# Moving the FFN token sums, a norm and the exps of Strassen groups to later slots of the program

## The chip, the cores and the metric

The kernel runs on one core of one Trainium2 chip. The metric is the device time of one execution in microseconds. Executions of one kernel lie within 0.5 to 4 us of each other here, so differences of one or two microseconds are judged from several rounds with an interval, not from single runs. The span that a profile shows is about 1.7 us shorter than the time of the same execution.

An engine (PE = TensorE, DVE = VectorE, ACT = ScalarE, POOL = GpSimd) runs its instructions in program order in these traces: in before, a sum that waited 5.28 us at the head of DVE's queue held up all DVE work behind it. SP issues nearly all DMA transfers of this kernel, also in program order (f4 below swaps two in the program, and the trace swaps them too), so a transfer whose data is not ready holds up those behind it.

## The reference

Two blocks, each behind a layer norm, on 2048 tokens of width 1024:

```
h  = x + linear_attention(layernorm(x)) @ wo        # 32 heads, phi(t) = where(t > 0, t+1, exp(t)) + 1e-6
h2 = h + (relu(g) * u) @ W_down                     # g, u = layernorm(h) @ W_gate, W_up ; width 3584
```

## The kernel before

The kernel is one long program in five stages: key/value projections, query projections, output projection (mixed with late attention tiles), gate and up products, down product. Most products use a Strassen scheme: seven products for eight, paid with sums of the operands and of the results. One group `sgroup` of seven products:

```python
a, f, b = alloc_bank(pool), alloc_bank(pool), alloc_bank(pool)
prod(a, X(0, 0), W(0, 0), True, "P1");  ident_act(bank(b), bank(a), ...)      # fk1: ACT copies PSUM to PSUM
hook(1)                                   # work of the group before (pend[1]), then a hook of the caller
prod(f, SX(2), TW(2), True, "P7");      ident_act(atmp, bank(f), ...)         # s7
hook(2)
... P6 -> fk2, hook(3), P2 -> e11 (exp on ACT, then min/add and max on DVE), hook(4) ...
prod(c, SX(0), TW(0), False, "P5");     ident_act(btmp[:, 0, :], bank(c), ...)  # sc
s22 = e22(...);  s22[0]()                 # DVE add
hook(5)
prod(b, X(1, 1), TW(3), False, "P4")
for f_ in s22[1:2]: f_()                  # exp of block (1,1), on ACT
s21 = e21(...);  s21[0]()                 # DVE add
for f_ in s22[2:]: f_()                   # min/add and max of block (1,1), on DVE
hook(6)
prod(c, SX(3), W(1, 1), False, "P3")
pend[1] = list(e12(...));  pend[2] = list(s21[1:2]);  pend[3] = list(s21[2:])
hook(7)
```

For keys and queries the four results go through phi; for values they are copied or added. A k group and a v group alternate; layer norms and operand sums of later tiles hang on the v group's hooks.

The output projection stage. `a2(t)` is the attention of a tile: matmuls, three DVE operations, then the transpose DMA T3d. `a4(t)` is the projection of a tile: 16 matmuls, residual add on DVE into a ring of three, store of h, then for the first eight tiles the statistics on ACT (two passes) and a chain of five small POOL operations. `a4_norm` is the norm on ACT and the transpose DMA T5d into `hnT`, the FFN's input. `s_sums` are the four Strassen sums over all of `hnT`, on DVE.

```python
LAG = NE                                   # 4
for t in range(NE, NST + LAG + 1):
    if LAG + 1 <= t < TPP + LAG + 1:
        a4_norm(t - LAG - 1)               # ACT norm, then T5d on SP
    if LAG <= t < NST + LAG:
        a4(t - LAG)
    if t < NST:
        a2(t)                              # ends with T3d on SP, read four steps later by a4(t)
    if t in (5, 7, 9, 11, 18, 19):
        load_w_next()                      # 512 KB of FFN weights, on SP
    if t >= 9:
        run(pool_t, 1)
    if 13 <= t < 17:
        s_sums()[t - 13]()
```

## Time and profile before

| | before |
|---|---|
| time, median | 761.73 us (761.55 to 762.08) |
| PE busy | 740.7 of 761.0 us |
| keys and values, to the first query product | 124.14 us |
| queries | 55.89 us (to 180.03) |
| output projection, to the first FFN product | 69.66 us (to 249.69) |
| FFN, to the end | 511.3 us |

Stage borders are read from the timeline of PE as starts of the first matmul with the next stage's tiles. The head and busy line of the page of before, and the engine shares of the chain that ended last:

```profile
span 761.0 us, 10079 instructions
PE 740.7 (97%) x3547; PEld 337.8 (44%) x3603; DVE 548.3 (72%) x1083; ACT 293.8 (39%) x500; POOL 84.5 (11%) x148
PE 89%; DVE 5%; ACT 3%; issue 2%; DMA 1%; DVEq 0%; POOL 0%; ACTq 0%; SPq 0%; POOLq 0%
```

PE is busy nearly always, so the change can only win PE's idle time and what PE loses at a lowered clock. The largest piece is in the projection stage. Timeline of before for PE there. The columns of a timeline are start and duration in us, engine, source line, operation, output<-input, shape, count, and in brackets the idle time in front and who ended it:

```profile
220.64 3.63 PE L602 MATMUL ps<-RW,RE 128*128 128x512 bf16 x15 [1.27 <-DMA RE<-RE]
...
224.62 3.63 PE L602 MATMUL ps<-RW,RE 128*128 128x512 bf16 x16
232.73 1.06 PE L602 MATMUL ps<-kvz,RAB 128*128 128x132 bf16 x8 [4.48 <-DVE RE L989]
```

RE<-RE is the attention transpose T3d. The long gap waits for DVE's line 989, an attention eviction. Timelines of before for DVE, ACT and the DMA queue of SP tell why that was late; line 1084 is a token sum, L1047 the norm, RH<-RXH its transpose T5d:

```profile
221.62 1.23 DVE L989 TENSOR_TENSOR RE<-ps,rden 128x1024 bf16<-128x1024 f32 x1
228.13 1.60 DVE L1084 TENSOR_TENSOR RC<-RH 128x2048 f16<-128x2048 bf16 x1 [5.28 <-DMA RH<-RXH]
...
218.18 1.24 ACT L1047 ACTIVATE RXH<-RXH,s 128x1024 bf16<-128x1024 bf16 x1 [1.43 <-POOL s L1037]
223.07 1.24 ACT L1047 ACTIVATE RXH<-RXH,s 128x1024 bf16<-128x1024 bf16 x1 [1.43 <-POOL s L1037]
...
224.34 1.24 SPq L512 DMA_TRANSPOSE RH<-RXH  x1
```

The sum stood at the head of DVE's queue 5.28 us, waiting for the last transpose. ACT's norms come every 4.89 us (223.07 minus 218.18), against 3.92 us of PE work per tile, because each norm waits 1.43 us for POOL. The windows view of before (window, busy time of each engine, PEclk, DMA share, GB/s) shows what the gap did to PE's clock:

```profile
227.04:230.96 3.92, 1.21 (x6) 0.36 (x4) 2.83 (x3) 0.00 (x0) 3.62 (x3) 1.00 1.14 249
230.96:234.88 3.92, 2.15 (x12) 1.32 (x13) 3.78 (x6) 0.00 (x0) 0.00 (x0) 0.55 1.06 309
234.88:238.80 3.92, 3.87 (x11) 1.49 (x11) 2.87 (x5) 0.00 (x0) 0.00 (x0) 0.57 1.08 235
```

A "busy" PE at a granted clock of 0.55 does little more than half the work. The Trainium skill ("TensorE: Matmul & The Clock Gate", Part 1) describes just this: an idle window halves the clock until the array has been busy for a while; the trace agrees: in windows of 0.1 us the clock is 0.50 from 231.39 to 238.22, which is 6.83 us.

In the key/value stage DVE has hardly any slack. DVE of before at the start of a v group (the v group's first product starts on PE at 73.28); the second and third line are the min/add and the max of a phi:

```profile
73.35 0.69 DVE L839 TENSOR_TENSOR RX<-ps,RXH 128x512 f32<-128x512 f32 x1
74.01 0.29 DVE L644 TENSOR_SCALAR RX<-RX 128x512 bf16<-128x512 bf16 x1
74.34 0.69 DVE L647 SCALAR_TENSOR_TENSOR RE<-RX 128x512 bf16<-128x512 f32 x1
75.52 0.29 DVE L644 TENSOR_SCALAR RX<-RX 128x512 bf16<-128x512 bf16 x1 [0.49 <-ACT RX L640]
```

And PE's waits of before between 60 and 110 us (total, times, longest):

```profile
PE ps L602 <- ACT RX L607: 2.2, 2, 1.3
PE ps L602 <- ACT ps L607: 0.7, 2, 0.4
```

### The profile page before, as it was taken

How to read it: one execution, taken by the hardware profiler on the slowest of the kernel's cores; microseconds unless marked ns; L12 is line 12 of the kernel's file. 1: busy time of each engine (PE TensorE's matmuls, PEld its weight loads, DVE VectorE, ACT ScalarE, POOL GpSimd, SP SyncE). 2: the span in 40 equal slices, each digit the busy share in tenths (PEclk: the TensorE clock that was granted, in tenths of full speed). 3: DMA queues.
4: the chain of work that ended last, by engine and by line, in shares of the span. 5: the costliest groups of instructions: out<-in, count | busy, mean ns of one | idle time of the engine just before them, and what ended most of it. 6: DMA issues, size and time to landing. Idle time of an engine off the chain costs nothing.

```text
span 761.0 us, 10079 instructions
## 1 busy us (share of the span) xinstructions
PE 740.7 (97%) x3547; PEld 337.8 (44%) x3603; DVE 548.3 (72%) x1083; ACT 293.8 (39%) x500; POOL 84.5 (11%) x148
## 2 busy tenths in 40 slices
PE   8999899999997999999999999999999999999998
PEld 3444344344543444444444444444444444444443
DVE  7978985889757698888886665847667686653343
ACT  4345455665650445454544100024454544420000
POOL 2656720000261000000000000000000000000000
PEclk9999999999998999999999999999999999999999
DMA  9643104212997777556545699753132332026664
GB/s 302 195 95 73 41 15 161 103 29 55 216 215 193 241 233 217 173 176 185 158 138 166 210 269 294 214 188 111 56 111 70 97 100 67 1 73 181 208 190 137
DMA packets 160225, 113.38 MB, mean 149 GB/s; under 512 B 51504, under 2 KB 141360, under 8 KB 160176
## 3 DMA queue, kind: packets, MB, share of 16 engines
q1 hardware_dynamic: 160176, 112.75, 51.5%
q8 instruction: 28, 0.46, 0.3%
q14 instruction: 21, 0.17, 0.1%
HBM read 85.46 MB, written 15.73 MB: 133 GB/s over the span
## 4 chain that ended last, share of the span: by engine, by line
PE 89%; DVE 5%; ACT 3%; issue 2%; DMA 1%; DVEq 0%; POOL 0%; ACTq 0%; SPq 0%; POOLq 0%
PE ps L602 89%; ACT ps L607 1%; ACT RX L640 1%; DVE RAB L647 1%; DVE RX L644 1%; DVE RX L839 1%; DVE RWG L764 1%; DMA RE<-RE 1%; ACT RXH L607 0%; DVE RE L900 0%; DVE RE L989 0%; DVE RXH L1008 0%; DVE st L615 0%; DVE rden L987 0%; DVE RXH L629 0%
## 5 line engine op out<-in xcount | busy, mean ns | idle before, releaser
L607 ACT ACTIVATE ps<-ps 128x512 f32<-128x512 f32 x150 | 87.5, 584 | 173.0 <-PE ps L602 155.6
L602 PE MATMUL ps<-RC,RO 128*128 128x512 f16 x672 | 154.2, 379 | 0.0
L602 PE MATMUL ps<-RW,RAB 128*128 128x512 f16 (+1 forms) x681 | 150.1, 379 | 0.6
L602 PEld LDWEIGHTS ps<-RW,RAB 128*128 128x128 bf16 (+1 forms) x692 | 67.7, 98 | 81.7
L602 PE MATMUL ps<-RH,RWG 128*128 128x512 bf16 x435 | 103.0, 379 | 0.7
L602 PEld LDWEIGHTS ps<-RC,RO 128*128 128x128 f16 x672 | 65.7, 98 | 79.3
L607 ACT ACTIVATE RE<-ps 128x512 f32<-128x512 f32 x120 | 71.1, 598 | 76.7 <-PE ps L602 54.5
L602 PE MATMUL ps<-RC,RWG 128*128 128x512 f16 x296 | 70.9, 379 | 0.7 <-ACT ps L607 0.7
L602 PEld LDWEIGHTS ps<-RH,RWG 128*128 128x128 bf16 x448 | 43.8, 98 | 52.9
L1171 DVE TENSOR_TENSOR RAB<-ps,RAB 128x512 bf16<-128x512 f32 x28 | 19.3, 691 | 65.1 <-PE ps L602 65.1
L602 PE MATMUL ps<-RW,RE 128*128 128x512 bf16 x248 | 59.1, 390 | 2.1 <-DMA RE<-RE 1.3
L602 PE MATMUL ps<-RH,RO 128*128 128x512 bf16 (+1 forms) x242 | 58.3, 379 | 0.7
L602 PE MATMUL ps<-RAB 128*128 128x512 bf16 x239 | 56.7, 379 | 1.3 <-ACT RAB L691 0.7
L607 ACT ACTIVATE RAB<-ps 128x512 bf16<-128x512 f32 x56 | 33.4, 597 | 62.0 <-PE ps L602 62.0
L1102 DVE TENSOR_TENSOR RO<-RWG,RO 128x512 f16<-128x512 bf16 x108 | 45.5, 421 | 1.8
L623 POOL TENSOR_TENSOR rstd<-ve,neghalf 128x1 f32<-128x1 f32 x24 | 14.8, 615 | 276.9 <-DVE ve L620 276.9
L602 PEld LDWEIGHTS ps<-RC,RWG 128*128 128x128 bf16 (+1 forms) x296 | 28.5, 98 | 36.6 <-ACT ps L607 3.1
L1178 DVE TENSOR_TENSOR RE<-ps,RE 128x512 f32<-128x512 f32 x56 | 38.4, 691 | 5.0 <-ACT RE L607 5.0
L615 DVE BATCH_NORM_STATS2 st<-RE 128x6 f32<-128x512 bf16 x48 | 30.7, 681 | 13.9 <-DMA RE<-h_scr 13.1
L1102 DVE TENSOR_TENSOR RO<-RWG 128x512 f16<-128x512 bf16 x108 | 40.7, 418 | 0.0
L602 PEld LDWEIGHTS ps<-RW,RE 128*128 128x128 bf16 x256 | 25.0, 100 | 31.3 <-issue 3.0
L602 PEld LDWEIGHTS ps<-RH,RO 128*128 128x128 f16 (+1 forms) x256 | 24.5, 98 | 31.1 <-ACT RX L607 2.6
(112 smaller groups left out, 808.1 us busy)
## 6 DMA issues: line engine op xcount, KB each, us to landing
RWG<-in_B_W_gate_dram SPq DMA_DIRECT2D x28, 512.0 KB, 3.7
RWG<-in_B_W_up_dram SPq DMA_DIRECT2D x28, 512.0 KB, 4.7
RW<-t_scr SPq DMA_DIRECT2D x56, 256.0 KB, 3.3
RW<-in_B_W_down_dram SPq DMA_DIRECT2D x42, 256.0 KB, 4.3
RW<-in_B_W_down_dram SPq DMA_DIRECT2D x14, 512.0 KB, 3.9
t_scr<-RW SPq DMA_DIRECT2D x14, 512.0 KB, 4.8
RE<-in_A_x_dram SPq DMA_DIRECT2D x23, 256.0 KB, 4.1
RAB<-in_A_wqkv_dram SPq DMA_DIRECT2D x8, 512.0 KB, 8.2
```

The source lines that it names most:

```text
L602: lambda e: e.matmul(out_ap, lhsT, rhs, start=start, stop=stop, skip_group_check=skip),
L607: PL.add("act", lambda e: e.activation(out=dst, in_=src, func=func), reads=reads, writes=writes, name=name)
L615: PL.add("dve", lambda e, c=c: e.bn_stats(out=st6[:, k, c * 6:(c + 1) * 6], in_=src_full[:, c * BCH:(c + 1) * BCH]), reads=[src_chunk_bufs ...
L623: PL.add("pool", lambda e: e.tensor_tensor(out=rstd[:, k, :], in0=ve[:, k, :], in1=neghalf[:], op=ALU.pow), reads=[B_ve[k], B_neghalf], wr ...
L640: PL.add("act", lambda e: e.activation(out=Et[:, k, :], in_=src, func=ACTF.Exp), reads=[src_buf], writes=[B_E[k]], name=name + "_exp")
L644: PL.add("dve", lambda e: e.tensor_scalar(out=Et[:, k, :], in0=Et[:, k, :], scalar1=1.0, scalar2=1e-6, op0=ALU.min, op1=ALU.add), reads=[] ...
L647: PL.add("dve", lambda e: e.scalar_tensor_tensor(out=dst_ap, in0=src, scalar=C1, in1=Et[:, k, :], op0=ALU.add, op1=ALU.max), reads=[src_bu ...
L764: PL.add("dve", lambda e: e.tensor_tensor(out=s(i), in0=in0, in1=in1, op=op), reads=reads, writes=[B_Sx[i][p]], name="Sx%d_%d" % (i + 1, p))
L839: PL.add("dve", lambda e: e.tensor_tensor(out=tmp, in0=p_, in1=s_, op=ALU.add), reads=[pb, sb_], writes=[tmp_buf], name=name + "_add")
L1102: PL.add(eng, lambda e: e.tensor_tensor(out=Tring[:, k, j], in0=in0, in1=in1, op=ALU.subtract), reads=reads, writes=[B_T[k][j]], name="T%d ...
L1171: PL.add("dve", lambda e: e.tensor_tensor(out=hh[:, f1, 0:SBW], in0=bank(BA[1]), in1=r11[:, rr, :], op=ALU.mult), reads=[B_bank[BA[1]], B_ ...
L1178: PL.add("dve", lambda e, w=w: e.tensor_tensor(out=ftmp[:, 4 + w, :], in0=bank(BF_[w]), in1=ftmp[:, 2 + w, :], op=ALU.add), reads=[B_bank[ ...
```

## The change

Its intent: let no engine wait at the head of its queue for something that will be ready a little later. Three parts, cut to the core (names of temporaries follow from it: s7 alternates between two buffers so that sums can be made in place):

```diff
 # 1. exps of a group issued in the next group's slots
-            ident_act(atmp, bank(f), [B_bank[f]], [B_at], name + "s7")
+            grp[0] += 1
+            s7, b7 = [(atmp, B_at), (btmp[:, 1, :], B_bt[1])][grp[0] % 2]
+            ident_act(s7, bank(f), [B_bank[f]], [b7], name + "s7")
...
             prod(b, X(1, 1), TW(3), False, "P4")
-            for f_ in s22[1:2]:
-                f_()
             s21[0]()
-            for f_ in s22[2:]:
-                f_()
...
-            pend[2] = list(s21[1:2])
-            pend[3] = list(s21[2:])
+            pend[2] = list(s22[1:])
+            pend[3] = list(s21[1:])
...
-                    hooks[3] = kvfin
+                    hooks[6] = kvfin
                 if r == 1:
-                    hooks[5 if ct == 0 else 3] = lambda t=ct: a2(t)
+                    hooks[6] = lambda t=ct: a2(t)
 # 2. norm of a tile behind the next one's statistics
+            if LAG <= t < NST + LAG:
+                a4(t - LAG)
             if LAG + 1 <= t < TPP + LAG + 1:
                 a4_norm(t - LAG - 1)
-            if LAG <= t < NST + LAG:
-                a4(t - LAG)
 # 3. token sums two tiles later
-            if 13 <= t < 17:
-                s_sums()[t - 13]()
+            if 15 <= t < 19:
+                s_sums()[t - 15]()
```

More of the change, by code (lines that the diff above doesn't have):

```diff
@@ L798, in sgroup @@
             prod(f, SX(2), TW(2), True, "P7")
-            ident_act(atmp, bank(f), [B_bank[f]], [B_at], name + "s7")
+            grp[0] += 1
+            s7, b7 = [(atmp, B_at), (btmp[:, 1, :], B_bt[1])][grp[0] % 2]
+            sc, bc = btmp[:, 0, :], B_bt[0]
+            ident_act(s7, bank(f), [B_bank[f]], [b7], name + "s7")
             hook(2)
@@ L809, in sgroup @@
             prod(c, SX(0), TW(0), False, "P5")
-            ident_act(btmp[:, 0, :], bank(c), [B_bank[c]], [B_bt[0]], name + "sc")
-            s22 = e22(bank(f), B_bank[f], btmp[:, 0, :], B_bt[0])
+            ident_act(sc, bank(c), [B_bank[c]], [bc], name + "sc")
+            s22 = e22(bank(f), B_bank[f], sc, bc)
             s22[0]()
@@ L814, in sgroup @@
             prod(b, X(1, 1), TW(3), False, "P4")
-            for f_ in s22[1:2]:
-                f_()
-            s21 = e21(bank(b), B_bank[b], atmp, B_at)
+            s21 = e21(bank(b), B_bank[b], s7, b7)
             s21[0]()
-            for f_ in s22[2:]:
-                f_()
             hook(6)
@@ L823, in sgroup @@
             pend[1] = list(e12(bank(c), B_bank[c]))
-            pend[2] = list(s21[1:2])
-            pend[3] = list(s21[2:])
+            pend[2] = list(s22[1:])
+            pend[3] = list(s21[1:])
             hook(7)
         pend = {}
+        grp = [0]
         def flush():
@@ L834, in flush, with add_phi @@
             pend.clear()
-        def add_phi(dst, dst_buf, tmp, tmp_buf, name):
+        def add_phi(dst, dst_buf, name):
             def go(p_, pb, s_, sb_):
                 def add():
-                    PL.add("dve", lambda e: e.tensor_tensor(out=tmp, in0=p_, in1=s_, op=ALU.add), reads=[pb, sb_],
-                           writes=[tmp_buf], name=name + "_add")
-                return (add,) + phi_steps(tmp, tmp_buf, dst, dst_buf, name)
+                    PL.add("dve", lambda e: e.tensor_tensor(out=s_, in0=p_, in1=s_, op=ALU.add), reads=[pb],
+                           writes=[sb_], name=name + "_add")
+                return (add,) + phi_steps(s_, sb_, dst, dst_buf, name)
             return go
@@ L889, in k_group @@
             sgroup(P1_POOL, True, X, SX, W, TW, pl(0, 0), pl(0, 1),
-                   add_phi(*dst(1, 0), btmp[:, 0, :], B_bt[0], "k_%d_0" % (2 * p + 1)),
-                   add_phi(*dst(1, 1), btmp[:, 1, :], B_bt[1], "k_%d_1" % (2 * p + 1)), "k%d" % p, hooks)
+                   add_phi(*dst(1, 0), "k_%d_0" % (2 * p + 1)),
+                   add_phi(*dst(1, 1), "k_%d_1" % (2 * p + 1)), "k%d" % p, hooks)
         def v_group(p, hooks=()):
@@ L932, in q_group @@
             sgroup(A_POOL[r], False, X, SX, W, TW, pl(0, 0), pl(0, 1),
-                   add_phi(*dst(1, 0), btmp[:, 0, :], B_bt[0], "q_%d_%d" % (r, ct)),
-                   add_phi(*dst(1, 1), btmp[:, 1, :], B_bt[1], "q_%d_%d" % (r, ct)), "q%d%d" % (r, ct), hooks)
+                   add_phi(*dst(1, 0), "q_%d_%d" % (r, ct)),
+                   add_phi(*dst(1, 1), "q_%d_%d" % (r, ct)), "q%d%d" % (r, ct), hooks)
         kv_started = [False] * 8
```

## The prediction

> **What bounds the kernel.** TensorE. The busy table gives PE 740.7 of 761.0 us (97%); the chain of waits is 89% PE. From about 249.5 us on (the FFN) the PE runs in regular 12.03-us pairs without gaps, and the change does not touch that. So only idle time before 249.5 us can be won, and all the change can win is far below 20 us.
>
> **Where PE idles (timeline and windows).**
> 1. Output projection + late attention, 180.0 to 249.5 us. Its matmuls need about 60.8 us (256 x 0.216 + 12 x 0.46) but take 69.5. One gap of 4.48 us stands at 228 us, released by DVE (L989): DVE had waited 5.28 us for the transpose DMA that completes hnT, at the head of its in-order queue with the first FFN token sum (1.60 us), and the projection's evictions stood behind it. After the gap the granted clock is 0.55 to 0.57 for about 8 us, as the Trainium skill says of an idle window ("TensorE: Matmul & The Clock Gate", Part 1); the trace agrees. Another 1.27-us gap (219 us) waits for a transpose.
> 2. Both come from ScalarE: each norm waits 1.43 us for the GpSimd chain of its own statistics, so a tile costs ACT 4.89 us against 3.92 us of PE, and T5d, then T3d on the same DMA queue fall behind.
> 3. Query groups, 124 to 180 us: about 4 us over the pure matmul time; DVE 8.3 to 9.5 of 10 us busy.
> 4. Key/value groups, 67 to 104 us: two pairs of 15.3 and 15.65 us instead of 13.5; DVE 9.3 to 9.65 of 10 busy.
>
> **What the change does.** No operation is added or removed; DVE, ACT and PE busy time should stay within 1%.
> - Norm behind the next statistics: ACT needs about 3.46 us per tile, so it keeps pace with PE; the last norm ends near 217 us instead of 224.3, hnT is complete near 221 instead of 228.1. Transposes for the projection are issued earlier.
> - Sums two tiles later: the first one starts near 229.5 us, hnT already there. The 4.5-us gap, the clock dip and most of the 1.27-us gap go: about -8.5 us. DMA is near full there (share 0.8 to 1.1), so a stall of a microsecond may remain.
> - Exps deferred: fk1 no longer waits behind the exp of the previous group. But fk2 still stands behind four ScalarE operations (0.25 us per query group stays), and DVE's work in the second half of the queries (about 7.06 us per group against 6.5 of PE) is the same, only its backlog moves into the projection. Query phase: -0.5 to -1.
> - Keys/values: the last min/add + max of each k group (0.98 us) moves into the v group, where DVE has 8 to 9 us of work, and leaves DVE idle about 1 us longer at the v group's start. There DVE is the limit, so this costs 0.5 to 0.8 us in each of three pairs: +1.5.
>
> **Sum:** 761.9 - 8.5 - 0.8 + 1.2 = about 753.8 us, range 750.0 to 757.5. Chances: faster by over 2% 0.05, within 2% 0.94, slower 0.01.
>
> **Signs.** Right: no DVE wait on the hnT transpose, no PE gap over 2 us after 180 us, clock 1.0 throughout, FFN start near 241 to 243 us, ACT no longer waiting 1.43 us on GpSimd per tile, pairs of the FFN still 12.03 us. The key/value pairs 0.5 us or more longer.
> **Wrong if:** transposes land later under the denser DMA traffic (PE waits on RE<-RE), the key/value deferral costs or wins several us, or hnT comes later than 229 us.

## The result

The changed kernel takes 759.1 us at the median (758.46 to 759.78) against 761.73. The ratio is 0.9965 (0.9948 to 0.9982). Ratios here are the mean time of one kernel's fast runs over that of the other's of the same rounds, so not quite the ratio of the quoted medians. That is 2.6 us won where about 8 were predicted, and outside the predicted range.

| stage, from the PE timelines | before | after | difference | predicted |
|---|---|---|---|---|
| keys and values | 124.14 | 126.46 | +2.3 | +1.2 (+1.5 in the text) |
| queries | 55.89 | 54.56 | -1.3 | -0.8 |
| output projection | 69.66 | 64.43 | -5.2 | -8.5 |
| FFN | 511.3 | 511.35 | 0 | 0 |
| span | 761.0 | 756.8 | -4.2 | -8.1 |

The profile of before happened to catch an execution of 762.71 us with the long clock dip (mean clock 0.995), that of after one of 758.46, the fastest of its four, so the differences of the table add up to 1.6 us more than the medians do. The page of after:

```profile
span 756.8 us, 10080 instructions
PE 737.7 (97%) x3547; PEld 337.2 (45%) x3603; DVE 545.6 (72%) x1083; ACT 291.2 (38%) x500; POOL 82.3 (11%) x148
```

Busy times are nearly the same: within 1%, but for POOL. Of the 4.2 us of span, 3.0 are PE's busy time, matmuls that no longer run at half clock (mean clock 1.0), and 1.2 are PE's idle time. In the projection stage the long gap is gone, the first sum starts at 232.35 without any wait, and the norms no longer wait for POOL, except the last one, 0.29 us instead of 1.43. PE, DVE and ACT of after:

```profile
221.75 3.63 PE L602 MATMUL ps<-RW,RE 128*128 128x512 bf16 x15 [0.60 <-DMA RE<-RE]
...
230.98 3.63 PE L602 MATMUL ps<-RW,RE 128*128 128x512 bf16 x15 [1.21 <-DMA RE<-RE]
235.09 10.52 PE L602 MATMUL ps<-RW,RE 128*128 128x512 bf16 x47 [0.49 <-DMA RE<-RE]
245.45 1.89 PE L602 MATMUL ps<-RH,RWG 128*128 128x512 bf16 x8
...
232.35 1.22 DVE L1084 TENSOR_TENSOR RC<-RH 128x2048 f16<-128x2048 bf16 x1
...
217.78 1.24 ACT L1047 ACTIVATE RXH<-RXH,s 128x1024 bf16<-128x1024 bf16 x1 [0.29 <-POOL s L1037]
```

PE waits for attention transposes instead. Why they are late shows in SP's queue of after. The last norm ended at 219.02, yet its transpose was issued at 224.80:

```profile
219.71 0.58 SPq L508 DMA_DIRECT2D h_scr<-RXH  x1
220.34 1.30 SPq L512 DMA_TRANSPOSE RH<-RXH  x1
221.75 1.25 SPq L512 DMA_TRANSPOSE RE<-RE  x1
223.04 0.58 SPq L508 DMA_DIRECT2D RWG<-in_B_W_up_dram  x1
223.72 0.56 SPq L508 DMA_DIRECT2D RE<-in_A_x_dram  x1
224.33 0.43 SPq L508 DMA_DIRECT2D h_scr<-RXH  x1
224.80 1.51 SPq L512 DMA_TRANSPOSE RH<-RXH  x1
226.42 2.49 SPq L512 DMA_TRANSPOSE RE<-RE  x1
```

Each issue follows the one before without a pause. From T3d of tile 6 to T3d of tile 12 (199.96 to 226.42 us) SP took 4.41 us per tile and was busy for 95% of that stretch; before, it was 4.95 us per tile, at 73%. The issues have also become longer: the last one above takes 2.49 us, where T3d took 1.29 to 1.68 in the same tiles of before. The last T5d landed 5.3 us after its issue began, at 230.1 us, against 228.1 before.

In the key/value stage, DVE of after at the start of the same v group (here the v group's first product starts at 74.00):

```profile
74.31 0.68 DVE L839 TENSOR_TENSOR RXH<-ps,RXH 128x512 f32<-128x512 f32 x1
76.23 0.29 DVE L644 TENSOR_SCALAR RX<-RX 128x512 bf16<-128x512 bf16 x1 [1.24 <-ACT RX L640]
...
79.82 0.76 DVE L644 TENSOR_SCALAR RX<-RX 128x512 bf16<-128x512 bf16 x1
80.61 1.11 DVE L647 SCALAR_TENSOR_TENSOR RE<-RXH,RX 128x512 bf16<-128x512 f32 x1
```

DVE idles 1.24 us where before it did a min/add and a max and idled 0.49. One more such pair now stands later in the v group, where POOL is busy: the pair at 79.82 takes 0.76 + 1.11 us, the same work took 0.29 + 0.69 us at 74.01 in the profile of before. The Trainium skill ("SBUF — State Buffer", "SBUF: two separate sides") says that DVE operations of certain kinds and GpSimd operations lock each other out of a shared port. The longer durations beside a busy POOL agree with that in part (the min/add at 76.23 took 0.29 us although POOL's records show it busy then too); no run here isolated it. PE's waits of after between 60 and 110 us grew from 2.9 to 4.7 us:

```profile
PE ps L602 <- ACT ps L607: 2.8, 3, 1.2
PE ps L602 <- ACT RX L607: 1.9, 2, 0.9
```

### The profile page after: what moved, and what is told of

It reads as the page before. It is cut to its first block, busy times and chain, and to the rows that moved or that the text cites. A ratio compares the mean times of both kernels' runs of the same rounds, so it can differ in the third digit from the quotient of the medians.

```text
span 756.8 us, 10080 instructions
## 1 busy us (share of the span) xinstructions
PE 737.7 (97%) x3547; PEld 337.2 (45%) x3603; DVE 545.6 (72%) x1083; ACT 291.2 (38%) x500; POOL 82.3 (11%) x148
## 4 chain that ended last, share of the span: by engine, by line
PE 84%; DVE 8%; ACT 2%; issue 2%; SPq 1%; DMA 1%; POOL 0%; DVEq 0%; ACTq 0%; POOLq 0%
PE ps L602 84%; ACT ps L607 1%; DVE RX L644 1%; DVE RAB L647 1%; SPq L512 1%; DVE RE L647 1%; DVE RE L989 1%; DVE RWG L764 1%; ACT RX L640 1%; DVE RE L900 1%; DMA RE<-RE 1%; DVE st L615 1%; DVE RX L839 0%; SPq L508 0%; DVE RXH L629 0%
## 5 line engine op out<-in xcount | busy, mean ns | idle before, releaser
L602 PE MATMUL ps<-RW,RE 128*128 128x512 bf16 x248 | 57.0, 379 | 2.8 <-DMA RE<-RE 2.3
L1178 DVE TENSOR_TENSOR RE<-ps,RE 128x512 f32<-128x512 f32 x56 | 38.4, 690 | 5.0 <-ACT RE L607 5.0
L644 DVE TENSOR_SCALAR RX<-RX 128x512 bf16<-128x512 bf16 x64 | 23.1, 361 | 22.3 <-ACT RX L640 22.3
L1183 DVE TENSOR_TENSOR RE<-ps,RE 128x512 f32<-128x512 f32 x56 | 38.1, 681 | 0.0
```

The source lines that it names most:

```text
L602: lambda e: e.matmul(out_ap, lhsT, rhs, start=start, stop=stop, skip_group_check=skip),
L644: PL.add("dve", lambda e: e.tensor_scalar(out=Et[:, k, :], in0=Et[:, k, :], scalar1=1.0, scalar2=1e-6, op0=ALU.min, op1=ALU.add), reads=[] ...
L1178: PL.add("dve", lambda e, w=w: e.tensor_tensor(out=ftmp[:, 4 + w, :], in0=bank(BF_[w]), in1=ftmp[:, 2 + w, :], op=ALU.add), reads=[B_bank[ ...
L1183: PL.add("dve", lambda e, w=w: e.tensor_tensor(out=ftmp[:, 6 + w, :], in0=bank(BB[w]), in1=ftmp[:, w, :], op=ALU.add), reads=[B_bank[BB[w] ...
```

## The experiments

Theory K: deferring the key groups' exps costs the key/value stage what the table shows. Theory Q: the late sums alone removed the gap; the rest of the hoped-for gain in the projection stage is lost because the transfers and their one issuing queue are full. Rival N, the prediction's own: ACT's lag is the root and the norm's place matters most. Each kernel was timed in several rounds against before on the same chip (five executions, or as many as are named); "stage" numbers are from its one profile.

### The three parts alone

**e1_sums.** Before, with part 3 only.

```diff
-            if 13 <= t < 17:
-                s_sums()[t - 13]()
+            if 15 <= t < 19:
+                s_sums()[t - 15]()
```

> The kernel before with one part of the change: the four FFN token sums two tiles later. Theory Q (the sums at the head of DVE's queue made the 4.5-us gap; the rest of what was hoped for is lost because the one DMA-issuing queue, SP, and the DMA engines are full): the gap and the clock dip go although ACT still waits 1.43 us per tile for GpSimd, the projection stage takes about 64.5 us instead of 69.6, total 756.5 to 758. Rival N (my prediction: ACT's lag is the root, the late sums alone only shift the wait): less than 2 us is won, total above 760.

Measured 758.77 us, ratio 0.9953 (0.9941 to 0.9965), projection stage 65.35 us. This one line wins at least as much as the whole change. ACT still waited 1.42 us per norm. ACT and PE of e1_sums:

```profile
223.61 1.24 ACT L1047 ACTIVATE RXH<-RXH,s 128x1024 bf16<-128x1024 bf16 x1 [1.42 <-POOL s L1037]
...
231.92 13.99 PE L602 MATMUL ps<-RW,RE 128*128 128x512 bf16 x64 [2.55 <-DMA RE<-RE]
```

The wait for DVE is gone; a wait of 2.55 us for a transpose stands in its place. The clock stayed at 1.00 after it in this profile, but two of the five executions had a mean clock of 0.997 and took 759.85 and 760.11 us, the other three 757.49 to 758.77. Rival N falls as the main cause.

**e2_norm.** Before, with part 2 only.

```diff
-            a4_norm ; a4 ; a2          # order in a step
+            a4 ; a4_norm ; a2
```

> The kernel before with one part of the change: the norm of a tile behind the next one's statistics. Theory Q: ACT keeps pace, but the last transpose of hnT is still issued near 224 to 225 us because SP needs over 4 us per tile to issue its transfers, so the first sum, two tiles earlier than in the changed kernel, still waits on the transpose: PE gap of 3 us or more, total within 1 us of before (761 to 762.5). Rival N: hnT complete by about 222 us, gap gone, total 754 to 757.

Measured 762.98 us, ratio 1.0002 (0.9990 to 1.0014), projection stage 70.23 us. ACT, SP and DVE of e2_norm: the last norm starts 7 us earlier than before, its transpose is issued only 0.42 us earlier, and the sum waits 6.66 us instead of 5.28.

```profile
215.94 1.24 ACT L1047 ACTIVATE RXH<-RXH,s 128x1024 bf16<-128x1024 bf16 x1 [0.29 <-POOL s L1037]
...
223.92 1.74 SPq L512 DMA_TRANSPOSE RH<-RXH  x1
...
229.22 1.23 DVE L1084 TENSOR_TENSOR RC<-RH 128x2048 f16<-128x2048 bf16 x1 [6.66 <-DMA RH<-RXH]
```

The time that ACT gained is spent in SP's queue (4.48 us per tile, busy 95%). Theory Q holds on this point.

**e3_groups.** Before, with part 1 only (the moved hooks included).

```diff
 # after, with parts 2 and 3 taken back
-            a4 ; a4_norm ; a2
+            a4_norm ; a4 ; a2
-                s_sums()[t - 15]()
+                s_sums()[t - 13]()
```

> The kernel before with the third part alone: exps of a Strassen group in the next group's slots, with the moved hooks. Theory K (the deferral leaves DVE idle at the start of each v group and puts its min and max into the fuller v group): first query product at 126.3 to 126.7 us instead of 124.1, query stage 1.0 to 1.5 us shorter, projection stage as before; total 762 to 763.5. Rival (the key/value loss comes only with the other parts, or is noise): first query product at 124.1 to 124.6, total 760 to 761.

Measured 763.92 us, ratio 1.0023 (1.0011 to 1.0035). The first query product came at 127.03 us, later than theory K's figure; queries took 54.34 us. This part by itself makes the kernel slower.

### Undoing the key deferral

**e4_k_early.** After, but the k groups keep block (1,1)'s exp, min/add and max in their own group (a flag `late22`, false for k groups).

```diff
             prod(b, X(1, 1), TW(3), False, "P4")
+            if not late22:
+                for f_ in s22[1:2]:
+                    f_()
             s21[0]()
+            if not late22:
+                for f_ in s22[2:]:
+                    f_()
...
-            pend[2] = list(s22[1:])
+            pend[2] = list(s22[1:]) if late22 else []
```

> The changed kernel, but the k groups' block (1,1) keeps its exp and its min/max in the same group as before the change; buffers, query groups and the projection stay changed. Theory K: first query product back at 124.0 to 124.6 us, total about 2 us below the changed kernel (756.5 to 757.5). Rival (the loss comes from the shared buffers of the alternating s7, or from exp21 one slot later): still 126 us, total 759.

Measured 756.90 us (6 runs), ratio 0.9927 (0.9916 to 0.9939); first query product at 124.28 us, queries 54.28. The key/value loss is gone with that one undo, and the query gain stays. Theory K holds: the deferral of the k groups is the cause. That DVE's idle start and its fuller v group are the way it acts is read from the traces; no run separates the two.

### What limits the projection stage now

All on top of e4, whose projection stage was 65.28 us (4.47 us per tile on SP).

**f1_late_w.** Two of the weight loads go later.

```diff
-            if t in (5, 7, 9, 11, 18, 19):
+            if t in (5, 7, 15, 16, 18, 19):
```

> On top of e4 (changed kernel, key exps early; projection stage 65.3 us, PE waits 2.9 us for attention transposes): two of the 512-KB FFN weight loads move from tiles 9 and 11 to tiles 15 and 16, behind the crowded part. Both forms of theory Q win: issue-limited (each load costs SP 0.58 us of issue): T5d and T3d come 1.2 us earlier near tile 12, 1 to 1.5 us won; engine-limited (1 MB is some 3 us of transfer at 300 GB/s): 2 to 3 us won, total 754 to 755. Rival (the transposes themselves are slow whatever else runs): nothing won.

Measured 754.28 us (4 runs), ratio 0.9897 (0.9884 to 0.9909), projection stage 61.78 us: by the ratios some 2.3 us better than e4, on the engine-limited side. The stage needs about 60.8 us of matmuls, so little is left to win in it. SP now takes 3.94 us per tile, PE's own pace. PE's waits from 180 to 250 us, first of e4_k_early, then of f1_late_w:

```profile
PE ps L602 <- DMA RE<-RE: 2.9, 4, 1.3
PE ps L602 <- DMA RE<-RE: 0.2, 1, 0.2
```

**f2_h_on_act.** The stores of h are issued by ACT.

```diff
-            dma(sl_hs[hs], h_scr[...], hsb[:, hs, :], "st_h_%d" % st, ...)        # PL.add("sp", ...)
+            PL.add("act", lambda e: e.dma_start(h_scr[...], hsb[:, hs, :]), ..., slot=sl_hs[hs], ...)
```

> On top of e4: the 16 stores of h (256 KB each) are issued from ScalarE's queue instead of SP's; same bytes, SP has 0.58 us less to issue per tile (some 4.4 to 3.8, below PE's 3.92). Issue-limited: SP's lag is gone, last hnT transpose issued by 220 instead of 223.3, PE waits for transposes under 1 us, 2 to 3 us won (754 to 755), unless the issue costs ACT itself 0.5 us per tile and makes its norms late. Engine-limited: PE waits for transposes stay 2 to 3 us, total within 1 us of e4.

Measured 755.76 us (4 runs), ratio 0.9916 (0.9903 to 0.9929), stage 63.77 us: between the two expectations. SP lost a 0.58-us issue per tile but its pace fell only from 4.47 to 4.22 us, because transposes took longer to issue. SP of f2_h_on_act:

```profile
211.14 0.58 SPq L508 DMA_DIRECT2D RWG<-in_B_W_gate_dram  x1
211.76 3.38 SPq L512 DMA_TRANSPOSE RH<-RXH  x1
```

The transpose behind a 512-KB load took 3.38 us to issue; at 224.34 in before it took 1.24.

**f3_h_split.** Each store of h in two halves: one more issue per tile, the same bytes.

```diff
-            dma(sl_hs[hs], h_scr[st * P:(st + 1) * P, :], hsb[:, hs, :], ...)
+            for hf in range(2):
+                dma(sl_hs[hs], h_scr[st * P + hf * 64:st * P + (hf + 1) * 64, :], hsb[hf * 64:(hf + 1) * 64, hs, :], ...)
```

> On top of e4: each store of h is cut into two of 128 KB; same bytes, one more issue of about 0.4 to 0.6 us per tile on SP. Issue-limited: SP falls behind by another 0.5 us per tile from tile 4 to 12, PE waits for transposes grow from 2.9 to 5 us or more, total 759 to 763. Engine-limited: total within 1 us of e4 (756 to 758).

Measured 759.08 us (6 runs), ratio 0.9959 (0.9945 to 0.9973), 4.77 us per tile. Total and pace are on the issue-limited side, though PE's waits for transposes (3.5 us) grew less than that side said. The edit does two things at once, though: each half also covers 64 partitions instead of 128, and no run separates that from the added issue. h1 below, where two added issues cost nothing measurable, speaks against a price on every issue.

**f4_t3_first.** In each step T3d ahead of T5d (`a4_norm` after `a2`).

```diff
-            a4 ; a4_norm ; a2
+            a4 ; a2 ; a4_norm
```

> On top of e4: in each step the attention transpose T3d is issued ahead of the norm's T5d instead of behind it; same operations and bytes. If T3d is late only because it stands in line behind T5d: PE waits for transposes fall below 1 us, 1 to 2 us won (755 to 756). If SP or the DMA engines are over-full in total, T5d now takes the lag and T3d still slips by tile 12: less than 1 us won.

Measured 756.24 us (6 runs), ratio 0.9924 (0.9910 to 0.9938): no difference from e4. A new order within a full queue wins nothing; the last T5d slipped to 225.44 (223.26 in e4).

**g1_late_w_no_norm.** f1 without part 2.

```diff
-            a4 ; a4_norm ; a2
+            a4_norm ; a4 ; a2
```

> Kernel f1 (keys early, two weight loads late; projection stage 61.8 us) with the norm back in front of the statistics. Theory (there were two limits one behind the other: ACT at 4.89 us per tile, then the DMA transfers at 4.2 to 4.4): with the DMA limit lifted, ACT's lag is the limit again, the last hnT transpose is issued near 224 us, the projection stage takes 64 to 66 us, total 757 to 758.5. Rival (the norm's place is worth nothing anywhere): total as f1, 754 to 755.

Measured 759.51 us, ratio 0.9962 (0.9948 to 0.9976), stage 67.51 us, more than expected. ACT is the limit again and SP is only 68% busy. ACT and PE of g1_late_w_no_norm:

```profile
223.25 1.24 ACT L1053 ACTIVATE RXH<-RXH,s 128x1024 bf16<-128x1024 bf16 x1 [1.43 <-POOL s L1043]
...
231.25 15.65 PE L602 MATMUL ps<-RW,RE 128*128 128x512 bf16 x62 [2.43 <-DMA RE<-RE]
```

So part 2, worth nothing alone, is worth some 5 us once the transfers have room (f1 against g1). Part of that is the clock: after the 2.43-us gap it was 0.50 for 3.41 us, and four of g1's five executions had a mean clock of 0.995 to 0.998 (759.40 to 760.95 us); the one at 1.0 took 757.81, against 753.68 to 754.73 of f1's at 0.999 or 1.0.

**g3_no_norm.** The same edit on e4, loads in their old places.

> Kernel e4 with the norm back in front of the statistics, weight loads in their old crowded place. Theory of two limits: ACT (4.89 us per tile) and DMA (about 4.4) are close, so taking the norm's part away costs 0 to 1.5 us: total 757 to 758.5. Rival (ACT's lag is what matters, as predicted at first): 3 us or more, 760.

Measured 758.02 us (6 runs), ratio 0.9949 (0.9936 to 0.9961), stage 67.57 us. Here part 2 is worth 0.0022 of the time, some 1.7 us. The profile is one of the two executions (759.69 and 760.41 us) with the clock dip, so its stage is longer than that of the other four (757.81 to 758.18).

**h1_late_w_tiny, h2_w_on_act, h3_f1_again.** f1 took two issues and 1 MB away at once. h1 puts two tiny transfers (2 KB each) where the loads stood; h2 leaves the loads in e4's place but issues them from ACT; h3 is f1 on the same chip.

```diff
 # h1, on f1
+            if t in (9, 11):
+                dma(sl_dum[(t - 9) // 2], warm[:].bitcast(bf16)[:, 0:8], xv[0:P, 0:8], "tiny_%d" % t, writes=[B_warm])
 # h2, on e4
-                load_w_next()
+                load_w_next("act" if t in (9, 11) else "sp")
```

> Kernel f1 with two tiny transfers (2 KB each, 128 rows of 16 bytes) issued from SP where the two weight loads stood (tiles 9 and 11): the issues are back, the megabyte is not. If the bytes were what stood in the way: total as f1 (754 to 755), attention transposes at 3.9 to 4.0 us per tile. If SP's issue time was: 1 to 2.5 us of f1's gain is lost, 755.5 to 757.

> Kernel e4 with the two weight loads of tiles 9 and 11 left in their places but issued from ScalarE's queue: the bytes stay, their two issues leave SP. If the bytes are what stands in the way: total as e4 (756 to 757.3), transposes still at 4.3 to 4.5 us per tile. If SP's issue time is: most of f1's gain comes, 754 to 755.2, transposes below 4.1 us per tile.

> Kernel f1 again on the same chip as h1 and h2, so that they can be set against it: 754 to 755, ratio 0.989 to 0.991.

Measured, four runs each: h1 753.91 us, ratio 0.9884 (0.9870 to 0.9899); h2 755.63, ratio 0.9905 (0.9889 to 0.9922); h3 753.77, ratio 0.9882 (0.9868 to 0.9897). h2 lies between its two expectations and h3 a little below its own. SP of h1_late_w_tiny shows the tiny issue at the length of a big one, and yet the time is f1's. SP's pace was 4.12 us per tile, not the 3.9 to 4.0 expected on the side of the bytes (3.93 in h3):

```profile
211.55 0.58 SPq L509 DMA_DIRECT2D warm<-in_A_x_dram  x1
212.17 1.19 SPq L509 DMA_DIRECT2D h_scr<-RXH  x1
213.41 1.28 SPq L513 DMA_TRANSPOSE RH<-RXH  x1
```

So the two issues alone do not take f1's gain back: what f1 took out of the way was first of all the megabyte. In h2's profile the long issues came back on SP, PE waited 2.5 us once and the stage took 65.75 us, as in e4:

```profile
209.27 3.16 SPq L512 DMA_TRANSPOSE RH<-RXH  x1
...
216.12 3.16 SPq L512 DMA_TRANSPOSE RE<-RE  x1
```

But that profile caught h2's slowest execution (757.59 us, mean clock 0.998): after the 2.5-us gap the clock was 0.50 for 3.41 us. The other three, at a mean clock of 1.0, took 755.29 to 755.82, about a microsecond better than e4's median and 1.7 us worse than h3. So with the megabyte in place the two issues may be worth about a microsecond; no profile of such an execution was kept, and e4 ran on another chip, so that stays open.

### The query stage, and the result once more

**g2_old_hooks.** e4 with `kvfin` and the first `a2` in their old slots (3 and 5).

```diff
-                    hooks[6] = kvfin
+                    hooks[3] = kvfin
-                    hooks[6] = lambda t=ct: a2(t)
+                    hooks[5 if ct == 0 else 3] = lambda t=ct: a2(t)
```

> Kernel e4 with kvfin and the first attention tiles back in their old slots of the query groups (slot 3 and 5 instead of 6). If the deferred exps alone made the query stage 1.3 us shorter: query stage 54.2 to 54.7 us, total as e4 (756.5 to 757.2). If the moved hooks did it: query stage 55.4 to 56 us, total about 758.

Measured 762.25 us (4 runs), ratio 1.0000 (0.9987 to 1.0013): neither expectation. The query stage took 60.31 us, longer than before the change. PE of g2_old_hooks:

```profile
168.35 1.04 PE L602 MATMUL ps<-RAB,RO 128*128 128x512 bf16 x4 [1.42 <-DVE RAB L647]
176.59 1.04 PE L602 MATMUL ps<-RAB,RO 128*128 128x512 bf16 x4 [1.43 <-DVE RAB L647]
```

Each next group's first product waits for a max on DVE. The deferral and the moved hooks belong together: with the exps deferred, DVE has the rest of the last group to do in the first slots, and an attention tile in slot 3 comes on top. What the new slots would win without the deferral was not run.

**g4_after_again.** The changed kernel again.

> The changed kernel again, beside the others on one chip, for a firmer figure: 758.5 to 759.7, ratio 0.996 to 0.997; its profile with the first query product at 126 to 127 us and PE waits of 2 to 4 us for attention transposes, so that neither is an accident of the first profile.

Measured 759.22 us (4 runs), ratio 0.9962 (0.9949 to 0.9974); first query product at 126.97 us, projection stage 64.62 us, PE waits of 2.5 us for transposes. The first profile was no accident.

### The best kernel

Kernel f1 is the changed kernel with the key deferral undone and two weight loads moved: 754.28 and, as h3, 753.77 us. It beats the changed kernel by some 5 us and before by some 8 to 9.

## Why the prediction was wrong

- **PE bounds the kernel, only idle time before 249.5 us can be won: right,** with the clock dip counted in, as the prediction did. The FFN took 511.3 us before and after.
- **The 4.48-us gap and its clock dip go: right.** No such gap in after, clock 1.0. But the reason that mattered was part 3 alone (e1), not the pair of parts that the prediction named as one step. "Both come from ScalarE" was wrong of this gap: in e1 ACT is as late as before, and the gap for DVE is gone; in e2 ACT keeps pace, and the gap stays (5.03 us).
- **"The last norm ends near 217 us ..., hnT is complete near 221 instead of 228.1. Transposes for the projection are issued earlier": the step from the norm to the transposes is the one that failed.** The norm ended at 219.02. The prediction in effect let the transposes follow at once, with issues as long as before. In after the last T5d was issued 5.78 us behind its norm, at 224.80 (before: 224.34), and hnT was complete at 230.1, later than before. T3d of tile 12 was issued at 226.42 (before: 226.81), and PE's waits for transposes rose from 1.3 to 2.3 us where the prediction allowed for a stall of about a microsecond.

  SP's queue was full: per tile a store (0.58), T5d (1.23), T3d (1.3) and, every second tile, a load (0.58 / 2) made 3.4 us in the profile of before, which would have fitted into PE's 3.92; in after the same issues took some 4.2 (95% of 4.41), because transposes took longer to issue. f1 and h1 show that without 1 MB of weight loads in that stretch PE's waits fall to 0.2 us or less. Why an issue lengthens beside a load is not shown. The prediction had seen a DMA share of 0.8 to 1.1, and two of its own "Wrong if" signs came: PE waits on RE<-RE, and hnT later than 229 us. The stage was mis-sized by 3.3 us (-8.5 against -5.2). Besides the 2.3 us for transposes it holds a wait of 0.58 us for DVE at its start, which before, e1 and e2 lack and e3 has (0.59): the backlog of the query groups, which the prediction named but gave no cost.
- **Keys and values: right in kind, too small in size.** Predicted +1.5 in the text, and carried into the sum as +1.2 by a slip; measured +2.3 and, in the second profile, +2.8. e4 shows that the deferral is the cause.
- **Queries: -1.3 instead of -0.5 to -1.** Right in kind, but the prediction did not mention the moved hooks, without which the deferral makes the stage 4.4 us longer than before (g2, 60.31 us).
- The rest of the difference is the profile's: the profile of before was an execution with the long clock dip (6.83 us instead of 3.41), so time read from it was partly not there in the median.

## What to carry to other kernels

When an engine is freed of a wait, ask what it feeds: here ACT's faster norms only filled a DMA queue that had 27% of slack, and that part, worth nothing alone, was worth some 5 us once the sums were late and 1 MB of unrelated loads was out of the way. Before moving work to a later slot, look at which slot its engine is idle in: moving DVE work out of an idle slot into a full one cost twice in these traces, once as the new idle time and once in the full slot. Before comparing two profiles, compare their mean clocks: one gap of 2.4 us or more could add a clock dip of 3.41 or 6.83 us, or none. Never let an engine's in-order queue reach an instruction whose input comes by DMA until a measured margin later; one line that does so (e1) was worth more than the rest of the change.

## What the Trainium skill lacked or had wrong

- "DMA: Bandwidth & Descriptors" gives the time that an issue holds its queue only as sequencer cycles of "previous generations", in a comparison with trn3, and not how it grows with the load; here it mattered: mostly 0.58 us for a plain transfer, whether 512 KB or 2 KB (stores took up to 1.32); 1.23 us for a transpose of a 128x1024 bf16 tile, and up to 3.38 us behind a 512-KB load. The same store issued from ACT mostly held that queue 0.33 to 0.35 us.
- The same page says (Rules for kernel authors) that spreading DMAs over SP, ACT and GpSimd doesn't help bandwidth and only saves issue time. Measured: a store per tile moved to ACT won a ratio of 0.0011, too little to be clear of the intervals, and longer transpose issues on SP took back more than half of the 0.58 us (the pace fell by 0.25). It agrees, but does not say that a transpose's issue lengthens with the load.
- "TensorE: Matmul & The Clock Gate", Part 1, lets the clock fall after at least one idle window of some 3.4 us. Here PE gaps of 2.39 to 2.50 us were enough in g1, g3 and h2, while one of 2.55 us in e1 left it at 1.00. The low clock then lasted 3.41 us (e3, g1, g3, h2) or 6.83 us (before, e2), which is one or two of the page's windows, and it came back 2.8 us (e3) to 5.5 us (before) after the matmuls began again; the page's statement that the window of 3413 ns runs freely, whatever the kernel does, fits these lengths.
